# Attention's weights turned unnormalised in the first 7 steps, with row sums formed by TensorE, in front of two feed-forward layers

## The chip, the cores and the metric

The kernel runs on one core of one Trainium2 chip. The metric is the device time of one execution in microseconds (us), the median of the runs shown. All arithmetic is 32-bit floating point; matmuls of the feed-forward layers use operands split into a high and a low part.

## What is computed

```python
# attention: q, k, v of shape (4 batches, 8 heads, 576 positions, 64)
scores = q @ k.T / sqrt(64) + slope[h] * -(i - j)
scores = where((i - j >= 0) & (i - j < 128), scores, -1e9)
attn = exp(scores - max(scores))
attn = attn / (sum(attn) + 1e-9)
x = (attn @ v), heads side by side            # 2304 tokens x 512
# first layer: softmax-gated, then normalised
h = x @ w_in                                  # 2304 x 1024
solu = h * softmax(h)
x = layernorm(solu) * g_ln @ w_out            # 2304 x 512
# second layer: gated
out = (silu(x @ w_gate) * (x @ w_val)) @ w_out2   # inner width 1536
```

## The kernel before, in words

The program is one long list of instructions for each engine. Their order comes from a planner in the kernel itself, the class `Emitter`: pieces of work are generators that yield requests (an engine or a choice of engines, a planned cost, what they wait for, an offset on their rank), and `Emitter.run` (L195) goes through planned time, gives each engine the ready request of the lowest rank, and emits it. The planned costs (`t_act`, `t_dve`, `t_pool`, `turn_by_dma`, L241 to L254) decide the order only; on the chip each engine works through its own list in order, and waits where an operand or a buffer isn't there. After a planned time (`TOGETHER`), `PATIENCE` says how long TensorE's tiled matmuls may be put off so that they come in one row.

Attention goes in 20 steps: 4 batches with 5 blocks of queries each (four of 128 and one of 64). A step has 4 units, each a pair of heads. For a unit, `score` (L428) has TensorE form the scores in a bank of PSUM, and `attend` (L468) does the rest:

- VectorE merges the two key blocks under the window with a predicated copy (L483), adds the bias and takes the maximum of each row in one custom instruction for each head (L488).
- ScalarE takes the exponential of each head (L493). It also accumulates the row's sum, which a second small instruction writes into the score bank.
- VectorE adds 1e-9 to the two sums and inverts them (L498, L499, `invert`); POOL, ScalarE or VectorE multiplies the weights by it (L504, L506, `normalize`). The score bank is free after `invert`.
- TensorE transposes the weights of both heads (L524), VectorE multiplies the late half by a triangular mask (L531), and ScalarE copies the other half out of PSUM (L534).
- After every second unit TensorE multiplies the values by the weights (L566, `values`), with the two heads in the two halves of the array's columns. The outputs of a step gather in one bank, `px`.

After the last unit of a step `px` is split into a high part (ScalarE or VectorE, L268) and what is left (VectorE, L272) into tiles `shared`, from which the up-projection `up` (L657) starts as soon as 128 tokens are there. `up`, the turning of its result (`flip`, by TensorE at L758 or, for tiles 4 to 13, by a copy in halves, L258 or L260, and a transposing DMA, L254) and `down1` (L771) are interleaved with attention; matmuls of both projections are at L653. The second layer follows: `products` (L992, matmuls L1007) and `steps_of` (L1152, matmuls L1169).

Weights arrive as 64-bit numbers and are decoded on the chip (`unpack`, L298): two ScalarE instructions (L306, L310), two on VectorE (L311, L312) and one on POOL (L314). This runs beside the first attention steps. All DMAs are issued by SP's queue, in order.

There are 8 PSUM banks, 5 buffers of weights `e`, 4 of turned weights `pt`.

Of the kernel before, what the change touches and what calls it, by code (L numbers as in the profile page):

```python
# [8 lines left out]
F32 = mybir.dt.float32  # L9
# [34 lines left out]
FLIP_BY_DMA = range(4, 14)  # L44
PLB = 2
PTB = 4
WHOLE = 20
# [12 lines left out]
O_EXP = -0.005  # L60
O_INV = 0.0
O_TURN = 0.136
O_PT = -1.188
O_VAL = 0.0
O_X = 0.316
# [3 lines left out]
O_FLIP = -1.299  # L69
O_LN = -0.416  # L70
O_SET = 0.102
# [3 lines left out]
TOGETHER = 96722.643  # L75
PATIENCE = 36.086
LEAST = 3
# [150 lines left out]
def attention_then_two_ffns(ctx: ExitStack, tc: tile.TileContext, qk, v, w_in, w_out, g_ln, w2, ident_d, base_d, tri_d, out):  # L228
# [12 lines left out]
    def t_act(n, sbuf=True, table=False):  # L241
        return (94 if sbuf else 51) + 94 * table + 0.833 * n
# [4 lines left out]
    def t_pool(n):  # L247
        return 149 + 2.104 * n
# [4 lines left out]
    def turn_by_dma(dst, src, nbytes, deps=()):  # L253
        return (DMA, max(445.0, nbytes / 250.0), lambda: nc.sync.dma_start_transpose(dst, src), deps, 2200.0)  # L254

    def halves_of(dst, src, n):
        words = src.bitcast(U16).rearrange("p (c h) -> p h c", h=2)
        return [(ACT, t_act(2 * n), lambda: nc.scalar.copy(dst, words)),  # L258
                (DVEP, t_dve(2 * n), lambda: nc.vector.tensor_copy(dst, words)),
                (POOL, t_pool(2 * n), lambda: nc.gpsimd.tensor_copy(dst, words))]  # L260

# [159 lines left out]

    e_s, pt_s, st_s, px_s = Slots(EB), Slots(PTB), Slots(EB), Slots(PXB)
    px_of, pts = {}, {}
    halved = [Done() for _ in range(NU)]
# [43 lines left out]
    def attend(u):  # L468
# [18 lines left out]
        for j in range(2):  # L487
# [3 lines left out]
            ds.append(d)  # L491
        for j, d in enumerate(ds):
            ex.append((yield (ACT, 93 + t_act(P, True, True), lambda j=j: nc.scalar.activation(  # L493
                e[0:n, j], e[0:n, j], AF.Exp, bias=st[0:n, j:j + 1], scale=-1.0,
                accum_out=sc[0:n, j:j + 1]), [d, ds[0]], 0.0, O_EXP)))

        def invert():
# [3 lines left out]
        def normalize(eng):  # L501
# [3 lines left out]
            else:  # L505
                eng.tensor_tensor(e[0:n], e[0:n], st[0:n, 6:8].unsqueeze(2).to_broadcast([n, 2, P]), ALU.mult)  # L506

        x = yield (DVE, 360, invert, ex, 0.0, O_INV)
        em.give(bank_s, x, k)
        x = yield ([(DVEP, t_dve(2 * P), lambda: normalize(nc.vector)),  # L510
                    (ACT, 2 * (93 + t_act(P)), lambda: normalize(nc.scalar)),
                    (POOL, t_pool(2 * P), lambda: normalize(nc.gpsimd))], [x], 0.0, O_INV)
        yield x
# [31 lines left out]
        if pr < size:  # L545
            yield px_s
            px_of[c] = yield bank_s
        else:
            yield started[u - size]
# [7 lines left out]
        def values():  # L557
# [3 lines left out]
            for r, late in todo:  # L561
                kp = n if late else P
                for j in range(2):
# [4 lines left out]
                                     skip_group_check=True)  # L568

        values.form = 2  # L570
        x = yield (PE, 100 + 450 * len(units), values, [loaded[c]], 0.0, O_VAL)
        for r in units:
# [8 lines left out]
        if t:  # L581
            em.give(v_s, x)
            em.give(vd_s, x)
        t0 = b * S + t * P
        done = 0
        last = []
        while done < n:
# [5 lines left out]
            hi, lo = (y[:, :, o:o + w] for y in x_tiles[i])  # L593
            src = px[:, :, done:done + w]
            y = yield (high(hi, src, 4 * w, False), [x], 0.0, O_X)
            y = yield (low(lo, src, hi, 4 * w, False), [y], 0.0, O_X)
            last.append((i, o + w, y))
# [5 lines left out]
        em.give(px_s, y)  # L603
        em.give(bank_s, y, px_of[c])
        valued[c].settle(y.time)
# [344 lines left out]
    def part_y(p, kk):  # L950
        yield opened2[p]
        if p == 1:
# [3 lines left out]
        src = yscr[p * 2 * NH:(p + 1) * 2 * NH, :, kk * 256:(kk + 1) * 256].rearrange("t h c -> (t h) c")  # L956
        x = yield (DMA, 2600.0, lambda: nc.sync.dma_start_transpose(
            r.rearrange("p (a h) t -> p a (h t)", a=2).bitcast(U16), src), (), 2000.0)
        if kk:
# [322 lines left out]
```

## Time and profile before

| | |
|---|---|
| median of 3 runs | 747.18 us (746.98 to 747.42) |
| the profiled execution, its own time | 744.56 us |
| its span, first to last instruction | 742.8 us |
| TensorE busy | 708.3 us, 95% of the span |
| VectorE (DVE) busy | 544.5 us, 73% |
| ScalarE (ACT) busy | 469.9 us, 63% |
| GpSimd (POOL) busy | 257.0 us, 35% |

In the profile PE is TensorE, PEld its loading of weights, and L12 is line 12 of the kernel before. A row of matmuls is given as start, duration and count; a 32-bit matmul of attention is two instructions in the trace. Instructions of one engine overlap at their ends, so that the distance from one start to the next is less than a duration.

### The profile page before, as it was taken

The page shows a single profiled execution, that of the slowest core. Times are in us where ns is not written, and L with a number is a line of the kernel's source. Part 1 is how long each engine was busy: PE and PEld are TensorE (multiplying, and loading weights), DVE is VectorE, ACT ScalarE, POOL GpSimd, SP SyncE. Part 2 cuts the span into 40 slices and gives each one's busy share as a digit, 9 for nine tenths or more (in the row PEclk, how much of TensorE's full clock was granted, in tenths as well). Part 3 has the DMA queues.
Part 4 walks back from the last instruction along what each step waited for, and adds up shares of the span by engine and source line. Part 5 has one row for each costly group of instructions (what it writes and reads, how often), then busy time and mean ns, then how long its engine had stood idle before and what let it go on. Part 6 is the DMA issues. An engine that isn't in the chain of part 4 may idle for free. (4 is left out here: it accounts for less than half of the span.)

```text
span 742.8 us, 14409 instructions
## 1 busy us (share of the span) xinstructions
PE 708.3 (95%) x5084; PEld 627.8 (85%) x5084; DVE 544.5 (73%) x1499; ACT 469.9 (63%) x1146; POOL 257.0 (35%) x268
## 2 busy tenths in 40 slices
PE   3879979999999999998999999999999999999997
PEld 1547757767787888888999999999999999999997
DVE  4778985667566654989978776876763699887975
ACT  7899996777777675786657555555553564442531
POOL 3686674454565554550034231221310000110200
PEclk9999999999999999999999999999999999999999
DMA  8763216354454327255564445643431788786851
GB/s 269 219 194 112 86 52 171 107 143 108 115 150 115 93 72 171 72 141 122 162 206 163 163 135 181 188 165 145 151 108 64 273 344 295 253 288 203 288 181 64
DMA packets 92329, 121.34 MB, mean 163 GB/s; under 512 B 46432, under 2 KB 59104, under 8 KB 92256
## 3 DMA queue, kind: packets, MB, share of 16 engines
q1 hardware_dynamic: 92256, 120.42, 51.6%
q8 instruction: 40, 0.66, 0.4%
q14 instruction: 33, 0.27, 0.1%
HBM read 76.09 MB, written 34.34 MB: 149 GB/s over the span
## 5 line engine op out<-in xcount | busy, mean ns | idle before, releaser
L1007 PE MATMUL bank<-yt,w 128*128 128x384 f32 x1008 | 183.5, 337 | 3.2 <-ACT t L1028 2.2
L1007 PEld LDWEIGHTS bank<-yt,w 128*128 128x128 f32 x1008 | 175.4, 188 | 6.4 <-ACT set L1028 2.8
L314 POOL TENSOR_TENSOR db<-db,dw 128x512 int32<-128x512 int32 x52 | 71.1, 1369 | 187.4 <-DVE db L312 144.4
L1169 PE MATMUL bank<-w,wo 128*128 128x384 f32 x756 | 132.9, 336 | 0.0
L1169 PEld LDWEIGHTS bank<-w,wo 128*128 128x128 f32 x756 | 132.3, 188 | 0.2 <-DVE w L272 0.2
L653 PE MATMUL bank<-wout,lnT 128*128 128x512 f32 x432 | 102.3, 392 | 0.0
L1007 PE MATMUL bank<-shared,w 128*128 128x384 f32 x504 | 96.0, 340 | 1.5 <-ACT set L1028 0.8
L653 PEld LDWEIGHTS bank<-wout,lnT 128*128 128x128 f32 x432 | 80.4, 188 | 17.2 <-issue 0.5
L1007 PEld LDWEIGHTS bank<-shared,w 128*128 128x128 f32 x504 | 87.2, 188 | 5.8 <-ACT set L1028 2.5
L653 PE MATMUL bank<-shared,shared 128*128 128x512 f32 x288 | 82.9, 418 | 1.6 <-ACT shared L268 1.6
L493 ACT ACTIVATE e<-e,st 128x128 f32<-128x128 f32 (+1 forms) x160 | 62.6, 401 | 14.7 <-DVE st L488 12.5
L653 PEld LDWEIGHTS bank<-shared,shared 128*128 128x128 f32 x288 | 51.9, 195 | 13.6 <-ACT shared L268 2.4
L506 POOL TENSOR_TENSOR e<-e,st 128x256 f32<-128x256 f32 (+1 forms) x66 | 40.8, 622 | 42.4 <-DVE st L499 31.1
L268 ACT CAST w<-t 128x768 fp32r<-128x768 f32 (+2 forms) x33 | 26.4, 806 | 42.3 <-DVE t L1123 26.7
L306 ACT ACTIVATE dw<-dw 128x512 int32<-128x512 uint32 x52 | 35.1, 675 | 14.5 <-DMA dw<-w 11.5
L488 DVE CUSTOM_DVE_ANT_0 e<-bank,bias 128x128 f32<-128x128 f32 (+1 forms) x160 | 38.5, 282 | 4.9 <-PE bank L454 2.7
L454 PE MATMUL bank<-keys,raw 64*32 64x160 f32 (+1 forms) x1152 | 32.5, 322 | 9.2 <-DMA keys<-qk 9.1
L1033 DVE TENSOR_TENSOR set<-set,bank 128x384 f32<-128x384 f32 x34 | 18.8, 552 | 30.3 <-PE bank L1007 23.3
L268 ACT CAST w<-db 128x512 fp32r<-128x512 f32 (+1 forms) x48 | 27.0, 565 | 20.7 <-POOL db L314 16.1
L524 PE MATMUL bank<-ident,e 128*128 128x128 f32 (+1 forms) x160 | 28.8, 291 | 11.3 <-POOL e L506 4.8
L653 PE MATMUL bank<-shared 128*128 128x512 f32 x144 | 38.9, 392 | 0.0
L524 PEld LDWEIGHTS bank<-ident,e 128*128 128x128 f32 (+1 forms) x160 | 18.3, 146 | 24.2 <-POOL e L506 8.7
(109 smaller groups left out, 1237.9 us busy)
## 6 DMA issues: line engine op xcount, KB each, us to landing
dw<-w SPq DMA_DIRECT2D x36, 512.0 KB, 3.9
t<-ascr SPq DMA_DIRECT2D x21, 768.0 KB, 5.5
ascr<-set SPq DMA_DIRECT2D x34, 384.0 KB, 2.6
later<-ascr SPq DMA_DIRECT2D x15, 768.0 KB, 5.4
wo<-wscr SPq DMA_DIRECT2D x6, 896.0 KB, 6.8
lscr<-pl SPq DMA_DIRECT2D x20, 256.0 KB, 2.3
raw<-qk SPq DMA_DIRECT2D x19, 256.0 KB, 3.4
yscr<-ys SPq DMA_DIRECT2D x18, 256.0 KB, 2.2
```

Of the source, the lines that this page charges most:

```text
L268: return [(ACT, t_act(n, sbuf), lambda: nc.scalar.copy(hi, src)), (DVEP if sbuf else DVE, t_dve(n, sbuf), lambda: nc.vector.tensor_copy(hi ...
L306: r = yield (ACT, t_act(512), lambda: nc.scalar.activation(a, lw, AF.Copy, scale=2.0 ** -29), (), 0.0, O_DEC)
L314: x = yield (POOL, t_pool(512), lambda: nc.gpsimd.tensor_tensor(b.bitcast(I32), b.bitcast(I32), a, ALU.add), [x, r], 0.0, O_DEC)
L454: nc.tensor.matmul(banks[ks[r]][i:i + Q, o:o + w], raw[c][rows, 2 * qd + j, i:i + Q], kt[rows, 2 * qd + j, k0:k0 + w], start=True, stop=True)
L488: d = yield (DVE, t_dve(P), lambda j=j: nc.vector.tensor_tensor_reduce(e[0:n, j], sc[0:n, j * 256:j * 256 + P], bias[0:n, 2 * pr + j, bs], ...
L493: ex.append((yield (ACT, 93 + t_act(P, True, True), lambda j=j: nc.scalar.activation(e[0:n, j], e[0:n, j], AF.Exp, bias=st[0:n, j:j + 1], ...
L506: eng.tensor_tensor(e[0:n], e[0:n], st[0:n, 6:8].unsqueeze(2).to_broadcast([n, 2, P]), ALU.mult)
L524: nc.tensor.transpose(tp[:, j, 0:n], e[0:n, j], ident[0:n, 0:n])
L653: nc.tensor.matmul(o, terms[m][0], terms[m][1], start=(m == 0), stop=(m == len(terms) - 1))
L1007: nc.tensor.matmul(o, l, r, start=first and m == 0, stop=m == 5, skip_group_check=True)
L1033: g2 = yield (DVE, t_dve(NH), lambda: nc.vector.tensor_add(t[:, 1], t[:, 1], sb), [x3, u2], 0.0, O_FREE)
L1169: nc.tensor.matmul(o, w[:, b], ob[k, i][a][:, j], start=i == 0 and m == 0, stop=i == HB - 1 and m == 2)
```

## The change

In the first `SUMS = 7` steps the exponential no longer accumulates its sum, and the weights are turned as they are. After the value matmuls of two units TensorE multiplies a tile of ones by the same turned weights, which puts each row's sum, repeated over 64 partitions, into a second bank that stands like `px`. At the end of the step 1e-9 is added while this bank is copied to a tile `rec` (by ScalarE or VectorE), VectorE inverts all of it (512 elements in each partition, 256 in the step of 64 queries) and multiplies it by `px`, and the split into high and low parts reads `rec` from SBUF, where POOL may form the low part too. The score bank is free after the maxima. Steps 7 to 19 are as before. Planned costs of two kinds of work and some offsets are other numbers.

```diff
+SUMS = 7
-O_INV = 0.0
+O_INV = 0.239
-O_VAL = 0.0
+O_VAL = -0.675
-O_LN = -0.416
+O_LN = -0.586
-PATIENCE = 36.086
+PATIENCE = 715.12
...
     def turn_by_dma(dst, src, nbytes, deps=()):
-        return (DMA, max(445.0, nbytes / 250.0), lambda: nc.sync.dma_start_transpose(dst, src), deps, 2200.0)
+        return (DMA, 1000.0 + 1.56 * src.shape[0], lambda: nc.sync.dma_start_transpose(dst, src), deps,
+                1300.0 + min(900.0, nbytes / 290.0))
...
-                (POOL, t_pool(2 * n), lambda: nc.gpsimd.tensor_copy(dst, words))]
+                (POOL, 450.0 + 0.3 * 2 * n, lambda: nc.gpsimd.tensor_copy(dst, words))]
...
+        if c < SUMS:
+            em.give(bank_s, ds[1], k)
+
+            x = []
+            for j, d in enumerate(ds):
+                x.append((yield (ACT, 93 + t_act(P, True, True), lambda j=j: nc.scalar.activation(
+                    e[0:n, j], e[0:n, j], AF.Exp, bias=st[0:n, j:j + 1], scale=-1.0), [d, ds[0]], 0.0, O_EXP)))
+            for x in x:
+                yield x
+        else:
...
         if pr < size:
             yield px_s
             px_of[c] = yield bank_s
+            if c < SUMS:
+                sum_of[c] = yield bank_s
...
+            if c < SUMS:
+                sums = banks[sum_of[c]].rearrange("p (r q) -> p r q", r=NPAIR)
+                for r in units:
+                    for j in range(2):
+                        nc.tensor.matmul(sums[j * 64:(j + 1) * 64, r, 0:n], ones, pts[c * NPAIR + r][:, 0, j, 0:n],
+                                         start=True, stop=True, skip_group_check=True)
...
+        if c < SUMS:
+            yield rec_s
+            rec = at.tile([P, NPAIR, P], F32, tag="rec", bufs=1, name="rec")
+            sums = banks[sum_of[c]].rearrange("p (r q) -> p r q", r=NPAIR)
+            y = yield ([(ACT, t_act(4 * n, False), lambda: nc.scalar.activation(rec[:, :, 0:n], sums[:, :, 0:n], AF.Copy, bias=1e-9)),
+                        (DVE, t_dve(4 * n), lambda: nc.vector.tensor_scalar_add(rec[:, :, 0:n], sums[:, :, 0:n], 1e-9))], [x], 0.0, O_X)
+            em.give(bank_s, y, sum_of[c])
+            y = yield (DVE, t_dve(4 * n), lambda: nc.vector.reciprocal(rec[:, :, 0:n], rec[:, :, 0:n]), [y], 0.0, O_X)
+            x = yield (DVE, t_dve(4 * n), lambda: nc.vector.tensor_mul(rec[:, :, 0:n], rec[:, :, 0:n], px[:, :, 0:n]), [x, y], 0.0, O_X)
+            em.give(bank_s, x, px_of[c])
+        src_x, in_sbuf = (rec, True) if c < SUMS else (px, False)
...
+            src = src_x[:, :, done:done + w]
+            y = yield (high(hi, src, 4 * w, in_sbuf), [x], 0.0, O_X)
+            y = yield (low(lo, src, hi, 4 * w, in_sbuf), [y], 0.0, O_X)
```

How this moves instructions shows at two places. The first is VectorE's queue between steps 0 and 1. Before, the decode of weights, the small sums and inverses of step 0 and then the predicated copies of step 1's scores follow each other:

```order
L311 TENSOR_SCALAR db<-db 128x512
L498 TENSOR_SCALAR st<-bank_82 128x2
L499 RECIPROCAL st<-st 128x2
L312 SCALAR_TENSOR_TENSOR db<-dw,db 128x512
L498 TENSOR_SCALAR st<-bank_83 128x2
L499 RECIPROCAL st<-st 128x2
L311 TENSOR_SCALAR db<-db 128x512
L483 COPY_PREDICATED bank_80<-tri,bank_80 128x2x128
L483 COPY_PREDICATED bank_81<-tri,bank_81 128x2x128
```

In the change (whose lines have other numbers: L488 is the predicated copy, L493 the maximum, L614 and L615 are new):

```order
L313 TENSOR_SCALAR db<-db 128x512
L314 SCALAR_TENSOR_TENSOR db<-dw,db 128x512
L614 RECIPROCAL rec<-rec 128x512
L488 COPY_PREDICATED bank_81<-tri,bank_81 128x2x128
L615 TENSOR_TENSOR rec<-rec,bank_86 128x512
L493 ISA e,st<-bank_81,bias 128x128
L493 ISA st 128x1
```

The large inverse of step 0 now stands ahead of step 1's first predicated copy, and the multiplication ahead of its first maximum.

The second place is TensorE's queue around the last transposes of step 4 (`bank<-ident,e 128x64`). Before, up-projections (`shared`) stand between the transposes and the value matmuls (`pt`):

```order
L524 MATMUL bank_83<-ident,e 128x64 x2
L524 MATMUL bank_82<-ident,e 128x64 x2
L524 MATMUL bank_87<-ident,e 128x64 x2
L653 MATMUL bank_85<-shared_74,shared_73 128x512 x4
L653 MATMUL bank_85<-shared_73,shared_74 128x512 x2
L566 MATMUL bank_87<-pt,vd 64x64 x4
L566 MATMUL bank_87<-pt,v 64x64 x4
L524 MATMUL bank_83<-ident,e 128x64 x2
```

In the change (L459 are scores, here those of step 5, L582 values, L590 the ones, L538 transposes):

```order
L459 MATMUL bank_86<-keys,raw 32x128
L459 MATMUL bank_85<-keys,raw 32x128
L582 MATMUL bank_84<-pt,vd 64x64 x4
L582 MATMUL bank_84<-pt,v 64x64 x4
L590 MATMUL bank_87<-pt,ones 64x64 x4
L538 MATMUL bank_83<-ident,e 128x64 x2
```

Up to this point TensorE's queue held 30 up-projection matmuls before and holds 12 in the change; step 5's 32 scores have moved ahead of it, and 36 of the 56 matmuls with ones are behind it.

## Rows read from the trace of the kernel before

**Rows 1.** Busy time by stretch: us, each engine's busy us (instructions), granted clock, DMA share, GB/s

```profile
0.00:20.00 20.00, 7.64 (x120) 4.09 (x128) 9.31 (x48) 14.61 (x47) 8.63 (x13) 1.00 0.83 267
20.00:52.00 32.00, 24.57 (x316) 15.03 (x305) 26.13 (x128) 27.94 (x96) 21.66 (x20) 0.99 0.64 192
...
60.00:100.00 40.00, 36.73 (x394) 26.93 (x394) 35.07 (x150) 37.98 (x116) 30.85 (x34) 1.00 0.35 105
100.00:120.00 20.00, 18.87 (x168) 14.15 (x167) 15.79 (x67) 17.27 (x58) 13.77 (x16) 1.00 0.24 77
120.00:300.00 180.00, 178.84 (x1629) 141.28 (x1628) 110.67 (x492) 128.25 (x385) 93.83 (x113) 1.00 0.46 122
```

**Rows 2.** Waits of TensorE, 0 to 100 us: waiting line, waited for, us, times, longest

```profile
PE bank L524 <- POOL e L506: 4.3, 4, 1.6
PE bank L524 <- ACT e L504: 4.0, 5, 1.3
```

**Rows 3.** Timeline of ScalarE and TensorE: start, us, line, operation, [idle before, releaser]

```profile
12.34 0.67 ACT L306 ACTIVATE dw<-dw 128x512 int32<-128x512 uint32 x1 [0.16 <-DMA dw<-w_in]
...
17.93 1.32 PE L454 MATMUL bank<-keys,raw 64*32 64x160 f32 x32 [1.84 <-DMA keys<-qk]
...
37.43 0.77 PE L454 MATMUL bank<-keys,raw 64*32 64x160 f32 x32
```

**Rows 4.** Costliest groups, shapes apart: line, operation, count, busy, mean ns, idle before

```profile
L493 ACT ACTIVATION_READ_ACCUMULATOR e<-e,st 128x1 f32 x128 | 20.3, 158 | 0.0
...
L499 DVE RECIPROCAL st<-st 128x2 f32<-128x2 f32 x64 | 10.6, 166 | 2.2
...
L498 DVE TENSOR_SCALAR st<-bank 128x2 f32<-128x2 f32 x64 | 10.0, 156 | 12.0 <-ACT e L493 11.5
...
L272 DVE TENSOR_TENSOR shared<-bank,shared 128x256 fp32r<-128x256 f32 x20 | 8.1, 418 | 1.5 <-ACT shared L268 1.2
...
L272 DVE TENSOR_TENSOR shared<-bank,shared 128x512 fp32r<-128x512 f32 x8 | 5.5, 684 | 1.0 <-ACT shared L268 1.0
```

**Rows 5.** Timeline of VectorE, 45 to 52.1 us

```profile
45.36 0.75 DVE L311 TENSOR_SCALAR db<-db 128x512 uint32<-128x512 uint32 x2
...
47.23 0.41 DVE L531 TENSOR_TENSOR pt<-bank,tri 128x256 f32<-128x256 f32 x1
47.56 0.68 DVE L272 TENSOR_TENSOR shared<-bank,shared 128x512 fp32r<-128x512 f32 x1
48.16 0.15 DVE L498 TENSOR_SCALAR st<-bank 128x2 f32<-128x2 f32 x1
...
48.62 0.48 DVE L483 COPY_PREDICATED bank<-tri,bank 64x128 f32<-64x128 uint32 x2
49.02 0.27 DVE L488 CUSTOM_DVE_ANT_0 e<-bank,bias 64x128 f32<-64x128 f32 x1
...
49.23 0.28 DVE L488 CUSTOM_DVE_ANT_0 e<-bank,bias 64x128 f32<-64x128 f32 x1
...
52.07 0.07 DVE L488 DVE_READ_ACCUMULATOR2_ANT st<- 64x1 f32 x1
```

**Rows 6.** Timeline of TensorE, 54.7 to 61 and 66.9 to 68.9 us

```profile
54.80 0.44 PE L566 MATMUL bank<-pt,vd 128*64 128x128 f32 x4
...
55.82 0.73 PE L653 MATMUL bank<-shared,shared 128*128 128x512 f32 x2
...
60.26 0.33 PE L524 MATMUL bank<-ident,e 64*128 64x64 f32 x2
...
66.94 1.65 PE L653 MATMUL bank<-shared,shared 128*128 128x512 f32 x6
68.43 0.60 PE L758 MATMUL bank<-ident,e 128*128 128x128 f32 x4
```

**Rows 7.** Waits of TensorE, 90 to 112 us

```profile
PE bank L524 <- ACT bank L695: 1.6, 1, 1.6
PE bank L653 <- ACT shared L268: 1.6, 2, 1.1
```

More of the change, by code (lines that the diff above doesn't have):

```diff
@@ L422, in attention_then_two_ffns @@
     e_s, pt_s, st_s, px_s = Slots(EB), Slots(PTB), Slots(EB), Slots(PXB)
-    px_of, pts = {}, {}
+    px_of, pts, sum_of = {}, {}, {}
+    rec_s = Slots(1)
+    ones = at.tile([P, 64], F32, name="ones")
+    nc.vector.memset(ones, 1.0)
     halved = [Done() for _ in range(NU)]
@@ L491, in attend @@
             ds.append(d)
[L492 to L495, printed above, removed]
         def invert():
@@ L506, in normalize @@
                 eng.tensor_tensor(e[0:n], e[0:n], st[0:n, 6:8].unsqueeze(2).to_broadcast([n, 2, P]), ALU.mult)
[L508 to L512, printed above, removed]
+        if c < SUMS:
[7 more added lines that the diff above has]
+        else:
+            for j, d in enumerate(ds):
+                ex.append((yield (ACT, 93 + t_act(P, True, True), lambda j=j: nc.scalar.activation(
+                    e[0:n, j], e[0:n, j], AF.Exp, bias=st[0:n, j:j + 1], scale=-1.0,
+                    accum_out=sc[0:n, j:j + 1]), [d, ds[0]], 0.0, O_EXP)))
+            x = yield (DVE, 360, invert, ex, 0.0, O_INV)
+            em.give(bank_s, x, k)
+            x = yield ([(DVEP, t_dve(2 * P), lambda: normalize(nc.vector)),
+                        (ACT, 2 * (93 + t_act(P)), lambda: normalize(nc.scalar)),
+                        (POOL, t_pool(2 * P), lambda: normalize(nc.gpsimd))], [x], 0.0, O_INV)
         yield x
@@ L568, in values @@
                                      skip_group_check=True)
+            if c < SUMS:
[4 more added lines that the diff above has]
+                                         start=True, stop=True, skip_group_check=True)
         values.form = 2
-        x = yield (PE, 100 + 450 * len(units), values, [loaded[c]], 0.0, O_VAL)
+        x = yield (PE, 100 + (450 + 220 * (c < SUMS)) * len(units), values, [loaded[c]], 0.0, O_VAL)
         for r in units:
@@ L593, in attend @@
             hi, lo = (y[:, :, o:o + w] for y in x_tiles[i])
-            src = px[:, :, done:done + w]
-            y = yield (high(hi, src, 4 * w, False), [x], 0.0, O_X)
-            y = yield (low(lo, src, hi, 4 * w, False), [y], 0.0, O_X)
+            src = src_x[:, :, done:done + w]
+            y = yield (high(hi, src, 4 * w, in_sbuf), [x], 0.0, O_X)
+            y = yield (low(lo, src, hi, 4 * w, in_sbuf), [y], 0.0, O_X)
             last.append((i, o + w, y))
@@ L603, in attend @@
         em.give(px_s, y)
-        em.give(bank_s, y, px_of[c])
+        em.give(*((rec_s, y) if c < SUMS else (bank_s, y, px_of[c])))
         valued[c].settle(y.time)
@@ L956, in part_y @@
         src = yscr[p * 2 * NH:(p + 1) * 2 * NH, :, kk * 256:(kk + 1) * 256].rearrange("t h c -> (t h) c")
-        x = yield (DMA, 2600.0, lambda: nc.sync.dma_start_transpose(
-            r.rearrange("p (a h) t -> p a (h t)", a=2).bitcast(U16), src), (), 2000.0)
+        x = yield turn_by_dma(r.rearrange("p (a h) t -> p a (h t)", a=2).bitcast(U16), src, 786432)
         if kk:
```

## The prediction

> **What bounds the kernel now.** I read the busy time by stretch first, because a share over the whole span mixes stages. TensorE is busy 178.84 us of the 180 between 120 and 300 us, but only 7.64 of the first 20 and 24.57 of the next 32 [rows 1]. From 120 us on the kernel is TensorE's queue almost without gaps, so a delay or a gain made earlier is carried to the end whole, and so is any work added to that queue. The seven steps that the change touches lie within the first 100 us. There, between 20 and 52 us, ScalarE is the fullest engine (27.94 of 32), with VectorE close behind (26.13), and from 60 to 100 us ScalarE has 37.98 of 40 and VectorE 35.07 [rows 1].
>
> Next I asked what TensorE waited for up to 100 us: 4.3 us in transposes for POOL's normalisation and 4.0 for ScalarE's [rows 2]. So the normalisation costs at most 8.3 us of TensorE idle time, less what is late anyway: the scores of step 1 stand until 17.93 us waiting for their keys [rows 3], and whatever comes earlier in step 0 is worth nothing.
>
> Last, the costs of one instruction [rows 4] and, since VectorE's neighbours overlap, their pitch from start to start [rows 5].
>
> **What the change removes.** In 28 units: the two small VectorE instructions at 156 and 166 ns, ScalarE's accumulator read (56 times 158 ns, 8.8 us), and a normalisation [rows 4]. ScalarE is so some 9 us lighter, and a unit's way from exponential to transposes loses three instructions and their handings over. The copies in halves that move from ScalarE to POOL belong to the flips of tiles 4 to 13, which follow those tiles' up-projections; by then TensorE has no gaps, so I put them, the other DMA costs and PATIENCE at nothing. TensorE's work covers them; uncovered they would cost one late transfer, a few us.
>
> **What it adds to TensorE.** 56 matmuls with ones. Sixteen instructions of the same shape (the values of two units, two instructions a matmul) took 55.82 - 54.80 = 1.02 us [rows 6]. The eight matmuls of a step are as many, so six full steps and step 4 at half width come to 6.6 us where TensorE is full; 20 of the 56 come after the point that I balance at below.
>
> **What it adds to VectorE.** Per step one reciprocal and one multiplication over 512 elements. The multiplication is priced by the subtraction of that shape: 684 ns, pitch 48.16 - 47.56 = 0.60 us [rows 4, 5]. A large reciprocal is not in the trace; only one of 2 elements is. Two sizes of subtraction (684 and 418 ns for 512 and 256 elements) give 1.04 ns an element and 152 ns fixed [rows 4]. The 2-element reciprocal takes 166 ns against its neighbour's 156, so 5 ns more for each element: 512 x (1.04 + 5) + 152 = 3.24 us. Bounds: 0.69 if the difference is only a fixed one; 3.74 if all above 152 ns is per element (7 ns). I take 3.25, since the neighbour's 156 is just what 152 ns and two elements give, so that fixed parts seem alike.
>
> The Trainium skill, VectorE: DVE Perf Modes, section on the 8-slice pipeline, says that reciprocal is an iterative divide with a repeat count of 8; at eight cycles of 0.96 GHz an element that makes an estimated 4.4 us, and seven of them some 8 us more of VectorE than by my price. The row of 2 elements agrees in kind (slower than its neighbour), and no run here shows the large one.
>
> The planner's cost for it is that of any 512 elements, so its order leaves no room for the rest.
>
> **The walk to step 4.** I balance both kernels at the last transposes of step 4, on TensorE at 60.26 + 0.33 = 60.6 us before [rows 6].
> - The first reciprocal waits for step 0's sums. Their copy stands on ScalarE behind the decode that starts with its data at 12.34 us [rows 3] and then some 7.3 us of instructions of kinds that it has there before as well: the reciprocal starts at about 19.7 us, an estimate.
> - From it to the last maximum of step 4 VectorE's new order holds 3 reciprocals (9.75), 3 multiplications (1.8), 32 maxima at 0.21 (6.7), 12 full and 4 half predicated copies at 0.33 and 0.20 (4.8), 12 masked copies at 0.33 and a half one at 0.20 (4.2), 4 decode pairs at 0.94 and a half pair (4.1) and a reduction (0.6): 31.9 us. The pitches: 49.23 - 49.02, half of 49.02 - 48.62, 47.56 - 47.23 (also taken for the full predicated copy, of the same size), half of 47.23 - 45.36 [rows 5]. VectorE was idle 5.9 of 32 us there before [rows 1]; I keep half, 2.9, since ScalarE's chain is lighter. Last maximum: 54.5 us, against 52.1 before [rows 5].
> - Then come step 4's last exponential, transposes and the value matmuls ahead of them, for which I allow 2.5 us: 57.0, or 3.6 earlier than 60.6. Before, TensorE had up-projections between these transposes.
> - But its new queue holds 18 up-projection matmuls fewer up to there; six take 68.43 - 66.94 = 1.49 us [rows 6], so 4.5 us are still to be done. It has step 5's 32 score matmuls behind it already: two lots like that of 0.77 us at 37.43, less their overlap, 1.4 [rows 3]. Of the ones 20 matmuls remain, 16 of them full: 2.1.
> - From 90 to 112 us TensorE waited 1.6 us for ScalarE's squares and 1.6 for its casts [rows 7]; with ScalarE lighter I take half off, 1.6.
>
> SP's queue now issues a second weight load ahead of step 2's keys, and both need a decode buffer that POOL must free; TensorE comes to those scores only behind step 1's, which wait for the first reciprocal, and I count nothing for it.
>
> Sum: -3.6 + 4.5 - 1.4 + 2.1 - 1.6 = 0.0 us. It is made on the profiled execution, 744.56 us with a span of 742.8, which lies 2.6 below the median of 747.18; on the median it gives **747.2 us**.
>
> **Rivals.**
> - *VectorE keeps up, faster.* If the large reciprocal is cheap (0.69, pitch 0.60), the list shrinks by 3 x 2.65 = 8 us, and step 4 could end 8 us earlier: 739.2. For it: ScalarE, the fuller engine, and the 8.3 us of waits are what the change relieves. Against: the 5 ns an element, and that TensorE is itself slow there: scores that take 1.32 us at 17.93 take 0.77 at 37.43, with a granted clock of 1.00 (the level of 2.4 GHz) over the first 20 us and 0.99 over the next 32 [rows 1, 3]. Half of it kept gives 743.2.
> - *VectorE becomes the bound, slower.* Four reciprocals (steps 3 to 6: 3 x 3.25 + 1.7 = 11.4) and four multiplications (2.2) fall where VectorE had 4.9 us of 40 left [rows 1]; 12 pairs of small instructions (3.9) and five subtractions that move to POOL (2.1) go. Net 7.6: 2.7 us too much at a full load, and all 7.6 if the idle time was waiting that stays. In its queue maxima and predicated copies stand behind each reciprocal, ScalarE's exponentials wait for those, and TensorE's transposes for these. With 5 us the time is 752.2, with 7.6 it is 754.8. It decides where VectorE's busy share from 60 to 100 us passes some 95%. For it: the queue was ordered for a reciprocal a fifth as long. Against: up-projections are there for TensorE to do.
> - *The change doesn't do what it says*, if the sums went to another engine or the order after 120 us were another one: the new queues show the matmuls, and from the second feed-forward on almost the same order, so I give this no chance of its own.
>
> **Numbers.** My forecast has 0.50 (743.5 to 751), the faster rival 0.25, the slower one 0.25. A measurement can tell about 0.2%, 1.5 us, from no change. Of my forecast's half 0.14 lies below 745.7, 0.24 within, 0.12 above 748.7. So faster 0.39, same 0.24, slower 0.37. The range, 740 to 755.5, reaches to nearly the far end of both rivals and leaves out what is beyond.
>
> **What would show it.** Right: a RECIPROCAL 128x512 of 3 to 3.8 us; no transposes that wait for POOL before 90 us; VectorE over 90% busy from 20 to 52 us; ones at about 1 us a step; step 4's last transposes at 57 us. Wrong in size: these at 52 or before (the faster rival), or TensorE waiting several us for maxima or masked copies after 57 us (the slower). Wrong altogether: a sum of TensorE's gaps after 120 us that differs by over 2 us from before.

## The result, and the profile after

The changed kernel takes **755.74 us** (median of 4 runs, 754.47 to 757.38), the one before 747.30 beside it: ratio 1.0110, interval 1.0084 to 1.0137. It is slower by 1.1%. The forecast was 747.2 us, the range ended at 755.5, so the time lies just above it, on the side of the rival "VectorE becomes the bound". The profiled execution took 754.87 us, span 753.1, which is 10.3 us more than the span before. The medians differ by 8.4, since the profiled execution of the kernel before (744.56 us) lies 2.7 under its median; the account below is one of the two profiled executions.

Busy time by stretch, after, in the columns of [rows 1] (the stretch from 52 to 60 us stands here too, and its row from the kernel before behind it):

```profile
0.00:20.00 20.00, 10.41 (x152) 6.59 (x153) 10.79 (x48) 14.08 (x35) 6.97 (x10) 1.00 0.80 263
20.00:52.00 32.00, 22.68 (x355) 16.05 (x333) 31.33 (x99) 21.74 (x55) 17.90 (x15) 0.87 0.63 194
52.00:60.00 8.00, 6.68 (x118) 5.21 (x118) 5.88 (x15) 4.45 (x13) 4.32 (x4) 0.68 0.45 133
60.00:100.00 40.00, 36.66 (x303) 27.76 (x304) 34.15 (x109) 32.24 (x80) 23.95 (x25) 0.91 0.29 96
100.00:120.00 20.00, 16.70 (x164) 12.00 (x163) 18.56 (x64) 16.57 (x55) 11.21 (x13) 0.91 0.13 41
120.00:300.00 180.00, 179.36 (x1665) 142.52 (x1664) 112.89 (x520) 122.45 (x399) 104.74 (x125) 1.00 0.46 122
```

```profile
52.00:60.00 8.00, 8.00 (x54) 5.72 (x55) 5.03 (x19) 6.73 (x24) 3.80 (x6) 0.84 0.46 157
```

ScalarE is busy some 6 us less from 20 to 52 us and again from 60 to 100 us. VectorE is now busy 31.33 of the 32 us between 20 and 52, against 26.13, and TensorE only 22.68, against 24.57. From 120 us on TensorE has no more gaps than before, so all that was lost was lost ahead of it. The granted clock has changed as well: from 20 to 120 us it is under 1.00 in every stretch, where before it was clearly under 1.00 only from 52 to 60 us (0.84).

The groups of the added operations (line, operation, names, count, busy us, mean ns, idle before):

```profile
L614 DVE RECIPROCAL rec<-rec 128x512 f32<-128x512 f32 x6 | 20.1, 3344 | 3.1 <-ACT rec L611 3.1
L614 DVE RECIPROCAL rec<-rec 128x256 f32<-128x256 f32 x1 | 1.8, 1753 | 0.0
L615 DVE TENSOR_TENSOR rec<-rec,bank 128x512 f32<-128x512 f32 x6 | 4.1, 677 | 0.0
L590 PE MATMUL bank<-pt,ones 128*64 128x128 f32 x96 | 8.7, 310 | 0.0
L590 PE MATMUL bank<-pt,ones 128*64 128x64 f32 x16 | 1.0, 268 | 0.0
```

The reciprocals are 21.9 us of new work for VectorE. TensorE's waits from 0 to 130 us, after, to be held against [rows 2, 7]:

```profile
PE bank L459 <- DMA keys<-qk: 7.4, 2, 5.7
PE bank L538 <- ACT e L513: 6.2, 5, 4.3
PE bank L459 <- DVE rec L615: 3.9, 2, 2.7
PE bank L538 <- DVE rec L615: 2.7, 1, 2.7
PE bank L459 <- ACT rec L611: 1.7, 1, 1.7
PE bank L538 <- ACT db L312: 1.7, 1, 1.7
PE bank L538 <- DVE st L498: 1.6, 1, 1.6
```

The waits for POOL's normalisation are gone. In their place TensorE waits for the multiplication behind the reciprocal (L615, 6.6 us together), for the copy of the sums (L611), and for exponentials (L513), which follow VectorE's maxima: 6.2 us, of which 4.3 are one wait behind the first reciprocal, where before the same transposes waited 4.0 us for ScalarE's normalisation (L504). The place that the prediction rested on shows how. VectorE's timeline (start, us, line, operation):

```profile
53.67 0.07 DVE L493 DVE_READ_ACCUMULATOR2_ANT st<- 64x1 f32 x1
53.67 1.00 DVE L314 SCALAR_TENSOR_TENSOR db<-dw,db 128x512 uint32<-128x512 uint32 x1
...
57.25 3.33 DVE L614 RECIPROCAL rec<-rec 128x512 f32<-128x512 f32 x1
...
60.66 0.67 DVE L615 TENSOR_TENSOR rec<-rec,bank 128x512 f32<-128x512 f32 x1
```

and TensorE's over the same time:

```profile
58.27 0.40 PE L590 MATMUL bank<-pt,ones 128*64 128x64 f32 x8
61.39 0.47 PE L538 MATMUL bank<-ident,e 64*128 64x64 f32 x2 [2.71 <-DVE rec L615]
...
64.38 3.51 PE L687 MATMUL bank<-shared,shared 128*128 128x512 f32 x8
...
69.88 2.11 PE L687 MATMUL bank<-shared,shared 128*128 128x512 f32 x8
...
105.29 3.52 PE L687 MATMUL bank<-shared,shared 128*128 128x512 f32 x8
```

Step 4's last maximum is done at 53.74 us, but its last transposes run only from 61.39 to 61.86. The last 2.71 us before them TensorE waits for step 3's multiplication, which frees the bank that they write into and stands behind step 3's reciprocal. TensorE's queue holds up-projections behind those transposes, and they wait with them until 64.38. There eight of their matmuls took 3.51 us, where eight others of the same form took 2.11 at 69.88: from 50 to 70 us the granted clock was 0.66, so part of the time the lower level (1.2 GHz).

### The profile page after: what moved, and what is told of

The parts are those of the page before. It is cut to its first block, busy times and chain, and to the rows that moved or that the text cites. A ratio compares the mean times of both kernels' runs of the same rounds, so it can differ in the third digit from the quotient of the medians.

```text
span 753.1 us, 14522 instructions
## 1 busy us (share of the span) xinstructions
PE 716.5 (95%) x5196; PEld 638.5 (85%) x5196; DVE 563.2 (75%) x1460; ACT 455.4 (60%) x1069; POOL 256.8 (34%) x261
## 5 line engine op out<-in xcount | busy, mean ns | idle before, releaser
L519 ACT ACTIVATE e<-e,st 128x128 f32<-128x128 f32 (+1 forms) x104 | 40.2, 399 | 24.3 <-DVE st L493 20.9
L459 PE MATMUL bank<-keys,raw 64*32 64x160 f32 (+1 forms) x1152 | 31.4, 316 | 13.1 <-DMA keys<-qk 7.4
L493 DVE CUSTOM_DVE_ANT_0 e<-bank,bias 128x128 f32<-128x128 f32 (+1 forms) x160 | 38.0, 282 | 6.3 <-PE bank L459 3.9
L538 PE MATMUL bank<-ident,e 128*128 128x128 f32 (+1 forms) x160 | 28.3, 296 | 13.2 <-ACT e L513 6.2
L314 DVE SCALAR_TENSOR_TENSOR db<-dw,db 128x512 uint32<-128x512 uint32 x52 | 39.5, 762 | 0.6
L538 PEld LDWEIGHTS bank<-ident,e 128*128 128x128 f32 (+1 forms) x160 | 18.9, 149 | 24.7 <-ACT e L513 9.6
```

The source lines that it names most:

```text
L314: x = yield (DVEP, t_dve(512), lambda: nc.vector.scalar_tensor_tensor(b, hw, 0x80000000, b, ALU.bitwise_and, ALU.bitwise_or), [x], 0.0, O_DEC)
L459: nc.tensor.matmul(banks[ks[r]][i:i + Q, o:o + w], raw[c][rows, 2 * qd + j, i:i + Q], kt[rows, 2 * qd + j, k0:k0 + w], start=True, stop=True)
L493: d = yield (DVE, t_dve(P), lambda j=j: nc.vector.tensor_tensor_reduce(e[0:n, j], sc[0:n, j * 256:j * 256 + P], bias[0:n, 2 * pr + j, bs], ...
L538: nc.tensor.transpose(tp[:, j, 0:n], e[0:n, j], ident[0:n, 0:n])
```

## The experiments

Every kernel ran in turn with the kernel before on its chip. Span and busy time are those of one profiled execution, which lies up to 2.7 us off the median of its kernel; TensorE's idle time is the span less its busy time. The change stands in the table for comparison.

| kernel | median us | ratio to before (interval) | span | TensorE busy | idle |
|---|---|---|---|---|---|
| before | 747.3 | 1 | 742.8 | 708.3 | 34.5 |
| the change | 755.74 | 1.0110 (1.0084 to 1.0137) | 753.1 | 716.5 | 36.6 |
| cheap inverse | 742.70 | 0.9935 (0.9912 to 0.9958) | 740.9 | 711.9 | 29.0 |
| no ones | 758.95 | 1.0165 (1.0131 to 1.0200) | 757.2 | 713.5 | 43.7 |
| cheap inverse, no ones | 742.34 | 0.9930 (0.9906 to 0.9954) | 740.0 | 706.9 | 33.1 |
| ones twice | 761.90 | 1.0204 (1.0182 to 1.0226) | 762.4 | 725.9 | 36.5 |
| cheap in steps 0 to 2 | 750.08 | 1.0039 (1.0019 to 1.0059) | 749.9 | 715.6 | 34.3 |
| cheap in steps 3 to 6 | 747.17 | 1.0000 (0.9983 to 1.0016) | 743.6 | 712.3 | 31.3 |

**1. The reciprocal replaced by a product of the same shape.**

```diff
-nc.vector.reciprocal(rec[:, :, 0:n], rec[:, :, 0:n])
+nc.vector.tensor_mul(rec[:, :, 0:n], rec[:, :, 0:n], rec[:, :, 0:n])
```

> The large reciprocals of the changed kernel (six of 128x512 at 3.34 us in its trace, one of 128x256) are replaced by multiplications of the same tile (rec times rec, some 0.68 us); all queues are otherwise the same, instruction by instruction. This leaves out the inverse, so the output isn't the reference's. Theory A (VectorE's reciprocals hold up TensorE): about 18 us less VectorE work in the first 115 us, TensorE's waits for exponentials and for rec go, 742 to 748 us. Theory B (the added matmuls with ones are the cost, VectorE is beside the path): 754 to 757, as the changed kernel. Theory C (the planner's new numbers made a worse order): 754 to 757 too.

742.70 us: 13.0 less than the change, and faster than before. The queues' order is unchanged, so what made the change slow is the time that VectorE spends in the reciprocal. The product took 1132 ns on the mean, so 2.2 us were taken off each full step. Busy time by stretch:

```profile
20.00:52.00 32.00, 27.03 (x410) 19.66 (x394) 27.47 (x111) 24.17 (x63) 21.82 (x17) 0.84 0.71 213
...
60.00:100.00 40.00, 36.40 (x353) 27.41 (x338) 37.74 (x121) 37.03 (x99) 30.85 (x33) 1.00 0.26 81
100.00:120.00 20.00, 20.00 (x158) 15.34 (x157) 15.53 (x65) 16.46 (x51) 15.77 (x19) 1.00 0.26 74
```

VectorE is fuller from 60 to 100 us here (37.74) than in the change (34.15), and yet the kernel is faster by 13 us: how full VectorE was in that stretch tells nothing of the loss. The clock at 0.84 from 20 to 52 us doesn't stand in the way either.

**2. The matmuls with ones left out, the reciprocals kept.**

```diff
-nc.tensor.matmul(sums[j * 64:(j + 1) * 64, r, 0:n], ones, pts[c * NPAIR + r][:, 0, j, 0:n],
-                 start=True, stop=True, skip_group_check=True)
...
-y = yield ([(ACT, t_act(4 * n, False), lambda: nc.scalar.activation(rec[:, :, 0:n], sums[:, :, 0:n], AF.Copy, bias=1e-9)),
+y = yield ([(ACT, t_act(4 * n, False), lambda: nc.scalar.activation(rec[:, :, 0:n], px[:, :, 0:n], AF.Copy, bias=1e-9)),
```

> The 56 matmuls with ones are left out, and the copy that fed the reciprocal reads the bank of values instead of the bank of sums; the reciprocals stay. The weights are so not normalised. The planned costs, and with them the order, stay. Theory A: in steps 0 to 4 VectorE is the bound and the ones lie in TensorE's waits, so only those of steps 4 to 6 come off, 2 to 4 us: 751 to 754. Theory B: all of their work comes off, 7 to 10 us: 746 to 749. Theory C: 754 to 757.

758.95 us, slower still, by 3.2 us: none of the theories had that sign. 9.7 us of matmuls are gone, but TensorE's busy time falls by only 3.0, and its idle time grows by 7.1. The stretches show part of it (52 to 60, 100 to 120 us):

```profile
52.00:60.00 8.00, 6.02 (x100) 4.38 (x100) 6.74 (x17) 4.83 (x14) 4.27 (x4) 0.50 0.57 177
...
100.00:120.00 20.00, 14.18 (x133) 10.26 (x133) 16.89 (x49) 13.51 (x45) 9.58 (x11) 0.83 0.13 41
```

The granted clock is 0.50, the lower level throughout, from 52 to 60 us (and 0.97 from 20 to 52, against 0.87 in the change). With VectorE setting the pace, ones taken out leave a gap and not a gain. Where the rest is lost can be read: step 4's last transposes end at 60.67 us, 1.2 sooner than in the change, and behind them TensorE idles 20.0 us instead of 14.9, while it is busy as long as in the change (676.5 us against 676.3) although some 3 us of ones are gone from there. So later waits are longer and other matmuls slower; why, this run doesn't settle.

**3. The planner's numbers alone** (SUMS at 0: no step is divided afterwards, all the other numbers as in the change).

```diff
-SUMS = 7
+SUMS = 0
```

> The changed kernel with SUMS = 0: all 20 steps normalise as before, only the planner's numbers (offsets, PATIENCE, costs of copies in halves and of turning DMAs) are new. It computes the reference. Theories A and B: as before, 745.5 to 749. Theory C: 752 to 757.

747.82 us, ratio 1.0010 (0.9994 to 1.0026). The orders, the DMA costs and the copies that moved to POOL neither cost nor bring anything by themselves; the loss comes with the new arithmetic.

**4. The planner told what a reciprocal costs.**

```diff
-y = yield (DVE, t_dve(4 * n), lambda: nc.vector.reciprocal(rec[:, :, 0:n], rec[:, :, 0:n]), [y], 0.0, O_X)
+y = yield (DVE, 153 + 6.24 * 4 * n, lambda: nc.vector.reciprocal(rec[:, :, 0:n], rec[:, :, 0:n]), [y], 0.0, O_X)
```

> The changed kernel, with the planner told what a reciprocal costs (153 ns and 6.24 ns an element instead of 68 and 1.04), so that the queues are ordered for it; the same instructions are issued. If A holds because VectorE is full (its busy time alone): 752 to 756. If A holds because the order has no room for the reciprocals, so that urgent instructions stand behind them: 747 to 751. Theory B: 753 to 757.

754.14 us (752.50 to 755.11), ratio 1.0092 (1.0061 to 1.0122): some 1.6 us under the change, within the spread of the two. The order that the planner finds with the true price still holds all seven reciprocals, so a wrong price is not the main fault. VectorE is busy 37.85 of the 40 us from 60 to 100 in this run.

**5 and 6. The cheap product in steps 0 to 2 only, then in steps 3 to 6 only** (`c < 3`, `c >= 3`).

```diff
-nc.vector.reciprocal(rec[:, :, 0:n], rec[:, :, 0:n])
+nc.vector.tensor_mul(rec[:, :, 0:n], rec[:, :, 0:n], rec[:, :, 0:n]) if c < 3 else nc.vector.reciprocal(rec[:, :, 0:n], rec[:, :, 0:n])
```

> The reciprocal of steps 0 to 2 is replaced by a product of the same shape (the divisors of these three steps are then wrong numbers); the order of every queue stays, steps 3 to 6 keep their reciprocals. Replacing all of them gave 742.7 us, 13 us less than the change. Theory 1 (both places count: the 4.9 us that step 4's last transposes come late, and the 5.4 us behind them): about half comes back here, since the list that ends with step 4's last masked copy loses 3 x 2.7 us, so 747 to 750 us, and step 4's last transposes end by 58 us instead of 61.9. Theory 2 (only what is lost after 60 us counts, as the projections that are held ready fill TensorE before): 753 to 756 us. Theory 3 (TensorE's low granted clock between 50 and 70 us follows the waits of the first steps, and is the loss): the clock in 52 to 70 us rises from 0.66 to over 0.9 and the time falls to 744 to 747 us.

> The other half: only the reciprocals of steps 3 to 6 are replaced by the product (their divisors are wrong numbers), steps 0 to 2 keep theirs. Theory 1: the fourth one no longer stands at 57 us ahead of what frees the bank, and the three behind it are cheap, so 745 to 749 us, and together with the run above the gains add up to about 13 us. Theory 2: all of the gain is here, 742 to 744 us. Theory 3: 752 to 756 us, since the waits of the first steps stay, with the clock at 0.66 in 50 to 70 us as now.

750.08 and 747.17 us: gains of 5.7 and 8.6 over the change, 14.3 together against 13.0 for all seven. So both places count and they add up, as in theory 1 (the first run is 0.08 us above its upper end); neither theory 2 nor theory 3 holds. Step 4's last transposes, TensorE's timeline of the first and then of the second run:

```profile
54.77 0.47 PE L538 MATMUL bank<-ident,e 64*128 64x64 f32 x2 [2.82 <-DVE rec L615]
```

```profile
57.90 0.34 PE L538 MATMUL bank<-ident,e 64*128 64x64 f32 x2
```

and step 4's last maximum in the second, VectorE's timeline:

```profile
52.67 0.07 DVE L493 DVE_READ_ACCUMULATOR2_ANT st<- 64x1 f32 x1
```

In the first they end 6.6 us sooner than in the change, while its span is 3.2 shorter: the wait for the fourth multiplication is still there (2.82 us), and the later reciprocals take back the rest. In the second they end 3.6 us sooner, the wait is gone, and the span is 9.5 shorter, so 5.9 us come from behind that point. The clock from 60 to 120 us is 1.00 there, as in the run with all of them cheap, and was 0.91 in the change.

**7. Each matmul with ones issued twice.**

```diff
-nc.tensor.matmul(sums[j * 64:(j + 1) * 64, r, 0:n], ones, pts[c * NPAIR + r][:, 0, j, 0:n],
-                 start=True, stop=True, skip_group_check=True)
+for again in range(2):
+    nc.tensor.matmul(sums[j * 64:(j + 1) * 64, r, 0:n], ones, pts[c * NPAIR + r][:, 0, j, 0:n],
+                     start=True, stop=True, skip_group_check=True)
```

> Each matmul with ones is issued twice, with the second overwriting the first, 112 more and some 9.7 us more of TensorE at full clock; the order of all queues stays. The run without them came out slower (758.95 us, clock 0.50 in 52 to 60 us) than the change with them (755.7). Theory 1 (until 110 us TensorE waits for VectorE, so these matmuls lie in gaps, and more of them keep the granted clock up): 752 to 757 us, with a granted clock over 0.95 in 20 to 70 us. Theory 2 (they are work that the end waits for, and the slower run without them has another cause): 762 to 766 us.

761.90 us, 6.2 more than the change and practically theory 2. In the profiled execution (764.35 us, the slowest of the five) busy time grows by 9.4, idle time not at all (36.5). Theory 1 wanted a clock over 0.95 from 20 to 70 us; it is 0.84 from 20 to 52 us (0.87 in the change) and 0.79 from 52 to 60 (0.68). So these matmuls don't hold the clock up over the whole stretch, and where it did rise the kernel was no faster.

```profile
20.00:52.00 32.00, 26.29 (x403) 20.29 (x402) 27.63 (x80) 19.75 (x49) 15.93 (x13) 0.84 0.63 186
```

VectorE is busy only 27.63 of 32 us, against 31.33: in this run it waits. The copy of the sums that the reciprocal needs stands behind the ones; VectorE's longest wait for it, ahead of the first reciprocal, is 4.1 us, against 2.8 in the change:

```profile
DVE rec L615 <- ACT rec L612: 4.5, 2, 4.1
```

With it the first reciprocal starts 1.0 us later (20.68); by the third the delay is 4.0 (49.55), and where that comes from was not traced. Step 4's last transposes end 3.5 us later than in the change, at 65.39. So a first helping of ones costs nothing and a second is paid for.

**8. The fourth corner: cheap inverse and no ones** (edits 1 and 2 together).

> The fourth corner of two by two: the matmuls with ones are left out and the reciprocal is replaced by the product (divisors are wrong numbers); the order of all queues stays. With reciprocals, leaving the ones out gave no gain (758.95 us against 755.7) and doubling them cost 6 us. Theory 1 (beside the reciprocals the ones lie in TensorE's gaps; without them they are paid in full): 742.7 us less the ones' 9 us, 732 to 737 us. Theory 2 (they are cover in either case): 741 to 744 us. Theory 3 (the ones keep the granted clock up, so that without them it falls as in the run without ones): above 745 us, with a granted clock under 0.8 somewhere between 50 and 120 us.

742.34 us, against 742.70 with the ones: theory 2. Without them TensorE is busy 5.0 us less and idle 4.1 more. Taking the ones away gains nothing even where VectorE is not full: part of their time turns into waits, and other matmuls take longer (the clock is 0.79 from 52 to 60 us, against 1.00 in run 1).

**9. The sums of eight heads under one another, 128 elements to invert.**

```diff
-nc.tensor.matmul(sums[j * 64:(j + 1) * 64, r, 0:n], ones, pts[c * NPAIR + r][:, 0, j, 0:n],
-                 start=True, stop=True, skip_group_check=True)
+nc.tensor.matmul(sums[j * 64:(j + 1) * 64, 0, 0:n], ones[:, r], pts[c * NPAIR + r][:, 0, j, 0:n],
+                 start=r == 0, stop=r == NPAIR - 1, skip_group_check=True)
...
+nc.vector.reciprocal(inv[:, 0:n], sums[:, 0, 0:n])
...
+nc.tensor.matmul(sums[:, r, 0:n], pick[:, r].rearrange("p j d -> p (j d)"), inv[:, 0:n],
+                 start=True, stop=True, skip_group_check=True)
```

> The same sums in another form: the ones stand in 16 of the 64 columns only, another 16 for each pair, so that the sums of a step's eight heads lie under one another in 128 rows x 128 columns. VectorE then inverts 128 elements a row instead of 512 (an estimate from 3344 ns for 512 and 1753 ns for 256: about 0.95 us), and four matmuls of 128 columns with a table of ones and zeros spread the inverses over the 512 (some 1 us a step). ScalarE copies that, and the product follows as before. The 1e-9 is left out, as the largest term of each sum is 1. Theory 1 (the loss is VectorE's reciprocal): 742 to 748 us. Theory of TensorE's work (ones and what is added are paid): 749 to 753 us. Rival: the way over TensorE and ScalarE and back puts the product later behind the queue of each, and the banks are held longer: 748 to 752 us, with TensorE waiting for the product at each step.

746.90 us, ratio 0.9998 (0.9983 to 1.0013): 8.8 us better than the change, the same as before. The reciprocal is as cheap as estimated, but spreading the inverses costs TensorE 7.9 us, which makes it busy 5.5 us longer than with the cheap product, while its idle time (28.3) is as low:

```profile
L616 DVE RECIPROCAL inv<-bank 128x128 f32<-128x128 f32 x6 | 5.7, 955 | 4.1 <-PE bank L594 4.1
...
L620 PE MATMUL bank<-inv,pick 128*128 128x128 f32 x48 | 6.9, 288 | 0.4 <-DVE inv L616 0.4
L620 PE MATMUL bank<-inv,pick 128*128 128x64 f32 x8 | 1.0, 268 | 0.0
```

**10. The sums from the exponentials, spread by TensorE.**

```diff
+    accum_out=dn[c][0:n, pr, j:j + 1]), [d, ds[0]], 0.0, O_EXP)))
...
+y = yield (DVE, 170.0, lambda: nc.vector.reciprocal(dn[c][0:n], dn[c][0:n]), expd[c], 0.0, O_X)
...
+nc.tensor.matmul(sums[j * 64:(j + 1) * 64, r, 0:n], dn[c][0:n, r, j:j + 1].to_broadcast([n, 64]), ident[0:n, 0:n],
+                 start=True, stop=True, skip_group_check=True)
```

> A version meant to beat both. The sums are no longer formed by TensorE with ones: each exponential adds up its row as in the kernel before, into a small table (queries x 8 heads a step), and the weights stay unnormalised. VectorE inverts the table, 8 elements a row (like the 166 ns reciprocals before), once a step; eight matmuls of 128 columns with the identity, whose other operand is one inverse repeated 64 times, turn and spread it (56 matmuls in all instead of the change's 112); ScalarE copies it, and VectorE multiplies the values as in the change. The 1e-9 is left out. VectorE's list loses 23.5 us of reciprocals and TensorE's some 5 us of ones. If both were paid: 734 to 740 us. If only the reciprocal was: 741 to 745 us, as with the cheap product (742.7). If the copy, product and bank that the division needs cost as much as the normalising they replace: 745 to 749 us.

747.11 us, ratio 0.9994 (0.9978 to 1.0010). The expectation counted wrongly: a matmul of this type leaves two records, so 56 matmuls are 112 records, as many as the ones had, and TensorE is busy 714.2 us. VectorE's list did lose its long reciprocals (21.9 us of them, not 23.5; busy time 543.3 us), but the spreading now stands in TensorE's queue, and TensorE waits for VectorE there: by the list of waits 1.8 us once for a maximum (L493) ahead of the spreading and 1.4 us once for the inverses (L603) ahead of value matmuls.

**11. GpSimd forms the inverse, as a power of -1.**

```diff
-y = yield (DVE, t_dve(4 * n), lambda: nc.vector.reciprocal(rec[:, :, 0:n], rec[:, :, 0:n]), [y], 0.0, O_X)
+y = yield (POOL, t_pool(4 * n), lambda: nc.gpsimd.tensor_tensor(rec[:, :, 0:n], rec[:, :, 0:n], mone[:, 0:1].unsqueeze(2).to_broadcast([P, NPAIR, n]), ALU.pow), [y], 0.0, O_X)
```

> The sums as in the change, but their inverses are formed by GpSimd (each to the power -1, 128 x 512 elements, in place) instead of VectorE, with the planner's price for a GpSimd operation of that size. No row here shows that operation; GpSimd is busy for 18 of the 32 us from 20 to 52, and 24 of the 40 from 60 to 100. VectorE's list becomes even shorter than with the cheap product (742.7 us). If the power takes up to 3 us: 741 to 745 us, a version that beats both. If it takes 5 us or more, the product waits for it in VectorE's queue, ahead of the maxima of the next pair: 750 us or more, and 35 us more of GpSimd's time would show.

1270.85 us. One such power takes 82 us:

```profile
L616 POOL TENSOR_TENSOR rec<-rec,mone 128x512 f32<-128x512 f32 x6 | 491.6, 81930 | 0.0
```

**12. As 10, with the inverses repeated by GpSimd**, so that four matmuls spread them.

```diff
+wided = yield (POOL, t_pool(512), lambda: nc.gpsimd.tensor_copy(
+    wide[0:n], dn[c][0:n].unsqueeze(3).to_broadcast([n, NPAIR, 2, 64])), [y], 0.0, O_X)
...
+nc.tensor.matmul(sums[:, r, 0:n], wide[0:n, r].rearrange("p j d -> p (j d)"), ident[0:n, 0:n],
+                 start=True, stop=True, skip_group_check=True)
```

> As the run in which the exponentials add up their rows (747.11 us, profiled span 744.4), with the inverses of a step repeated 64 times by GpSimd into a table of 512 elements a row, ahead of the step's values in its queues, so that four matmuls with a 128-wide operand turn and spread them instead of eight with a 64-wide one: half the matmul records, 56 instead of 112, some 4.5 us less of TensorE, and its wait for the small reciprocal (1.4 us) goes. If TensorE's work is what keeps that version at the time of before: 742 to 745 us. If it is the copy, the product and the banks behind TensorE: 746 to 749 us.

745.39 us beside 746.82, ratio 0.9986 (0.9971 to 1.0001). TensorE is busy 710.0 us, 4.2 less than in 10, as expected. It is the best version here that computes what the reference does, but for the 1e-9, which 9, 10 and 12 leave out. It is 10 us under the change, but its interval still touches no change against the kernel before.

## Why the prediction was wrong

- **The price of the reciprocal held.** 3344 ns against 3.25 us forecast; with 1753 ns for half of it that is 6.2 ns an element and some 160 ns fixed. The Trainium skill, VectorE: DVE Perf Modes, section on the 8-slice pipeline, has a repeat count of 8 for it, from which the prediction worked out an estimate of 4.4 us; the measurement decides, and no run here bears eight cycles an element out.
- **The walk held as far as VectorE's list, in part by luck.** The first reciprocal came at 19.69 us (19.7 forecast) and the last maximum of step 4 at 53.74 (54.5). Between them VectorE was idle 0.7 us where 2.9 were kept, and its list took 33.3 us instead of 31.9: two misses that nearly cancel.
- **The first step that failed is "for which I allow 2.5 us: 57.0".** The transposes ended at 61.86, 8.1 us behind the last maximum, 4.9 later than forecast and 1.3 later than before. Two things stood in the way. The first is ScalarE's list, in order:

```profile
55.27 0.60 ACT L611 ACTIVATE rec<-bank 128x512 f32<-128x512 f32 x1 [1.08 <-PE bank L590]
...
57.36 0.27 ACT L548 COPY pt<-bank 128x128 f32<-128x128 f32 x1 [1.05 <-DVE pt L545]
57.52 0.40 ACT L513 ACTIVATE e<-e,st 64x128 f32<-64x128 f32 x1
```

Step 4's last exponential stands behind the copy of step 3's sums, which waits for the ones, and behind a copy of turned weights, and ends only at 57.92. Run 6 shows this part alone: with a cheap product in step 3 there is no wait for a bank, and the transposes still end 5.5 us behind the last maximum (58.24 against 52.74). The second is the bank: TensorE was through with the ones ahead of the transposes at 58.67, and waited 2.71 us more for step 3's reciprocal and multiplication (57.25 + 3.33, then the multiplication's end at 61.33), a fourth of each that the list did not count because they come after the last maximum.

- **The second is the -1.6 us for ScalarE's waits, and the third a term that the sum did not have: a slower clock.** TensorE from the end of step 4's last transposes to the end of the span, before, in the change and in run 6, whose queues are in the same order as the change's:

```profile
60.60:742.80 682.20, 667.49 (x4598) 602.54 (x4598) 503.43 (x1305) 420.05 (x980) 222.54 (x231) 1.00 0.51 159
61.90:753.10 691.20, 676.29 (x4592) 610.39 (x4592) 513.27 (x1293) 414.43 (x966) 227.24 (x234) 0.99 0.50 157
58.24:743.60 685.36, 671.67 (x4592) 607.63 (x4592) 509.13 (x1293) 414.14 (x967) 229.05 (x235) 1.00 0.51 159
```

TensorE's idle time there is 14.7 us before and 14.9 in the change: +0.2 where -1.6 was forecast. Its busy time is 8.8 us longer than before. Run 6 does the same 4592 instructions in 671.7 us, so 4.2 of the 8.8 are other work in the queue (forecast: 4.5 - 1.4 + 2.1 = 5.2), and 4.6 are the same work done more slowly. With the 1.3 at the transposes that is 1.3 + 4.2 + 4.6 + 0.2 = 10.3, all that the span grew by; since single executions of a kernel differ by some 2 us, the smaller terms are rough. Two lots of eight up-projection matmuls, at 64.38 and 105.29 us, took 3.51 and 3.52 us instead of 2.11, which is 2.8 of the 4.6. The slower clock goes with the reciprocals of steps 3 to 6: from step 4's last transposes to 120 us it is 0.92 in the change and 0.93 in run 5, which have them, and 1.00 in runs 1 and 6, which don't; run 5 takes 677.5 us for the same 4592 instructions, run 1 671.9. That the clock falls because TensorE waits for those reciprocals is argued from this, not shown.

- **The slower rival had the right engine, but not the path.** It named a chain (reciprocal, then maxima, exponentials, transposes) in steps 3 to 6 and 752.2 to 754.8 us; the measured 755.74 is 0.9 above its upper end. After 57 us TensorE waited only 0.25 us for an exponential, but 5.6 us for the multiplication (2.7 and 1.2) and the copy of the sums (1.7), and the slower clock had no place in it, so that the figure came near is in part luck. It also made the verdict hang on VectorE's busy share from 60 to 100 us passing 95%; it was 85%, and 94% in run 1, which is 13 us faster. Whether the place of each reciprocal in the queue or the load counts there is not separated: run 4, ordered with the true price, was as slow.
- **The faster rival's figure came out, in part by luck.** With a cheap inverse it gave 743.2 us, and run 1 measured 742.70. But it kept half of 8 us by judgement, and it priced an inverse of 0.69 us, where the product in run 1 took 1.13.
- **The ones were priced well where the clock is up, and taking them away gains nothing.** Those of a step are two rows of eight records; from start to next start one took 0.54 us at 94.43 and 1.00 at 54.09, so 1.1 to 2.0 us a step against 1.02 forecast. They are time in TensorE's queue, part of the 4.2 us above. Yet runs 1 and 8 differ by only 0.4 us with and without all of them, so they are not time that the end waits for: without them TensorE waits longer or its other matmuls run slower.
- **What was put at nothing for the planner's numbers was nothing:** alone they gave 0.1% (run 3).

Left open is why, beside full reciprocals, leaving out the ones made the kernel 3.2 us slower (run 2 shows where, not why), and why doubling them made it 6.2 us slower: the later copy of the sums accounts for 1.0 us of that at the first reciprocal.

## What to carry to other kernels

When work moves from many small instructions into one long one on an in-order engine, don't stop the count at the engine's total: look for what stands behind each long instruction at the moment it is issued, buffers that it frees included, and take the neighbouring step's instance into the walk. Price an operation that the trace shows only on tiny tiles by its difference from a like neighbour per element; that worked here within 3%. And find out whether added matmuls fall into gaps before charging them: replace the suspected cost by a cheap operation in the same place of the queue, which told in one run what no sum over busy shares did.

## What the runs showed of the hardware

- VectorE's reciprocal is linear in the elements of a row: 547, 955, 1753 and 3344 ns for 64, 128, 256 and 512 elements, so about 6.2 ns an element, where a subtraction of 512 elements took 684 ns [rows 4]. Laying the sums of a step's eight heads under one another, 128 elements a row instead of 512, made it 2.4 us cheaper (run 9).
- The power on GpSimd (POOL in the rows) took 82 us for 128 x 512 elements, 160 ns an element of a row; GpSimd's repeating copy to as many elements took 610 ns.
- Taking matmuls away made the kernel slower (run 2), with the granted clock at 0.50 from 52 to 60 us and 0.97 from 20 to 52; with twice as many (run 7) it was 0.79 and 0.84, against 0.68 and 0.87 in the change. The kernel with the cheap product was faster than the one before by 0.6% although its clock from 20 to 52 us was 0.84.
- The same 4592 TensorE instructions in the same order kept it busy 671.7 us in run 6 and 676.3 in the change, with the granted clock at 1.00 and 0.92 from their start to 120 us.
- The product in place, with all operands in SBUF, took 1132 ns on the mean (0.67 to 1.79 us) where the product with one operand from PSUM took 677; why was not tried.
